# Wider up products, a fused clamp, an earlier first norm and a new fillers' table in a one-core mLSTM, gMLP and channel-mix kernel

## The chip, the cores and the metric

The kernel runs on one core of a Trainium2 chip. The metric is device time in microseconds (us); lower is better. The kernel before has a median of 297.68 us over three runs (297.44 to 298.55).

## The reference, cut to what matters

Three layers follow one another. B = 2 batches, S = 768 tokens, H = 8 heads of D = 40, so 320 features.

```python
# 1: mLSTM recurrence, per batch and head
m_new = max(f_gate + m, i_gate)
C = exp(f_gate + m - m_new) * C + exp(i_gate - m_new) * v k^T
n = exp(f_gate + m - m_new) * n + exp(i_gate - m_new) * k
y_t = sigmoid(o_gate) * (C q) / max(|n.q|, 1.0)
# 2: gated MLP over x = y laid out (B, S, 320)
h = relu(x @ w_in)                      # 320 x 1024
u, v = h[..., :512], h[..., 512:]
v_n = (v - mean(v)) / sqrt(var(v) + 1e-6)
x = (u * (w_spatial @ v_n + b_spatial)) @ w_out
# 3: channel mix
k = relu(mix_k(x) @ w_k)                # 320 x 1024
out = sigmoid(mix_r(x) @ w_r) * ((k * k) @ w_v)
```

## The kernel before, in words

The recurrence is computed in chunks of 128 tokens. There are 12 chunks (6 for each batch), taken in the order of `SEQ` = 0, 6, 1, 7, 2, 8, 3, 9, 4, 10, 5, 11: the two batches alternate, and two neighbours of `SEQ` are a **pair** (pair 1 is chunks 0 and 6, pair 6 is 5 and 11). The code counts pairs from g = 0. Names carry the chunk: `x11` is the x of chunk 11.

For one chunk the steps are: `scores` (k times q, tile `sc`), `logd` (the decay exponents, tile `ld`, whose Exp ScalarE takes into `dt`, which VectorE multiplies by `sc`), `inter` (q times the carried state, `ip`), `state` (the state's update, `sp` into `cn`), `intra` (`dt` times v, tile `av`; it ends in two halves, tasks N0 and N1), and `normalise`. That last one is a chain: `nn` plus `av` (line 626, VectorE; line 627, ScalarE, for each batch's first chunk), the output gate `og` times `nn` on GpSimd (line 622), the denominator `dn` on VectorE (lines 621, 629, 631), `x` = `og` times `dn` (line 632) and a copy of 64 columns on GpSimd (line 635). `turn` then transposes `x` on TensorE (tile `tp`, line 653), and ScalarE and VectorE split the result into a high and a low part in `xg`, one slot of three for each pair.

Products of layers 2 and 3 run in split precision: high times high, high times low and low times high, eight or so matmuls into one accumulator (line 678, function `mm3`). `upart(g)` makes the u half of pair g: four feature blocks of eight matmuls with 256 tokens moving; ScalarE applies the relu twice (once for each batch, line 771). `vpart(i)` makes the v half of one chunk with its normalisation: relu into `vr` (line 747; two buffers), statistics (735, 738), the 1e-6 (line 739, VectorE), the power -0.5 (line 744, GpSimd), for the first five chunks a bias (line 751, VectorE), scale, cast, and the low part on GpSimd into `vn`. Two PSUM banks (tag `mm`) hold these products and six (tag `at`) all else.

The order of work is laid down when the program is built. A planner with a clock of its own holds a list of tasks for each position p (slots S0, I, T, N0, X, S1, N1), takes the first of the next four whose inputs it believes ready, and after each task of slot s issues `FILL[p][s]` matmuls out of the **fillers** (`upart` and `vpart`). Where it sees a gap and has no filler it issues junk matmuls (`heat`, tile `wp`, line 378). `LATE`, `load`'s rates and the numbers in the chains are its estimates. Every engine then runs its list strictly in order, and TensorE's is fixed. What is left of the fillers after the last task is issued in one stretch, and then `spatial` (tile `spp`) starts, whose first call needs all six `vn` of batch 0 and whose weight halves come from GpSimd (`wsp`).

At the start, all loads go through SyncE's queue, whose order is spelt in two strings: `f i d q b o0 o1` (f and i gates, the identity, q and k of chunk 0, a mask, the output gates of chunks 0, 6, 1 and 7) and then `q6 k0 k6 v0 v1 v2 n` (q and k of chunk 6, k, v and q of chunks 0 and 6, w_u in three parts, q and k of chunk 1). `open_gate` takes the sigmoid of the output gates on ScalarE (line 370); the next Exp there needs a new table (ACT_TABLE_LOAD).

## Time and profile before

| | |
|---|---|
| median of three runs | 297.68 us (297.44 to 298.55) |
| the profiled execution, its own time | 296.37 us |
| its span, first to last instruction | 294.6 us |
| outside the span in that execution | 1.77 us |
| busy share of the span: TensorE, VectorE, ScalarE, GpSimd | 98%, 75%, 60%, 46% |
| recurrence and fillers, to the first spatial product | 0 to 119.1 us |
| the rest, layers 2 and 3 | 119.1 to 294.6 us |

Times inside a profile are counted from the span's first instruction. PE is TensorE's matmuls, PEld its weight loads, DVE is VectorE, ACT ScalarE, POOL GpSimd, SP SyncE. A matmul's own duration overlaps that of its neighbours, because they are pipelined; the time from the start of one to the start of the next is what a place in the list costs.

### The profile page before, as it was taken

The numbers are of one execution on the slowest core, as the hardware profiler recorded it, in microseconds if no ns is written. First come the engines' busy times: TensorE is split into PE (matmuls) and PEld (weight loads), VectorE is DVE, ScalarE is ACT, GpSimd is POOL, SyncE is SP. The second block draws the span as 40 slices with busy tenths as digits, with TensorE's granted clock in tenths as the row PEclk, the third lists the DMA queues.
The fourth block names the chain that finished last, engine by engine and source line by source line (L and its number), as shares of the span: only waits on it lengthen the run. The fifth ranks groups of instructions, "written<-read, shape, count | busy, mean of one in ns | idle before, by whom it ended". The sixth has DMA issues, their size and how long they took to land.

```text
span 294.6 us, 5892 instructions
## 1 busy us (share of the span) xinstructions
PE 288.9 (98%) x2167; PEld 265.2 (90%) x2167; DVE 221.3 (75%) x451; ACT 176.2 (60%) x385; POOL 134.5 (46%) x153
## 2 busy tenths in 40 slices
PE   8999999999999999999999999999999999999995
PEld 6777999888887889999999999898999899988994
DVE  6688898887778767366989989977986896556211
ACT  7676698947766456534454754694793788146400
POOL 5235426255776757424736526283812580045100
PEclk9999999999999999999999999999999999999999
DMA  6999697482412132462314302311102000100011
GB/s 153 312 233 299 179 296 211 108 234 77 128 49 74 53 92 62 162 191 103 89 47 148 112 6 83 93 43 44 49 0 87 4 0 22 47 22 1 2 45 46
DMA packets 14374, 29.53 MB, mean 100 GB/s; under 512 B 2641, under 2 KB 8017, under 8 KB 14345
## 3 DMA queue, kind: packets, MB, share of 16 engines
q1 hardware_dynamic: 14217, 29.09, 33.3%
q8 instruction: 17, 0.28, 0.4%
q0 software_dynamic: 128, 0.07, 0.2%
q14 instruction: 12, 0.10, 0.1%
HBM read 26.95 MB, written 1.97 MB: 98 GB/s over the span
## 4 chain that ended last, share of the span: by engine, by line
PE 82%; DVE 6%; ACT 5%; POOL 3%; DMA 2%; SPq 1%; issue 1%; DVEq 0%; POOLq 0%; ACTq 0%
PE spp L678 17%; PE kp L678 15%; PE vv L678 14%; PE up L678 8%; PE wop L678 8%; PE rp L678 5%; PE av L607 3%; PE vp L678 3%; PE sc L476 2%; PE ip L578 2%; DMA og<-in_o_tok_dram 2%; PE sp L541 1%; POOL vn L238 1%; DVE sb L735 1%; PE tp L653 1%
## 5 line engine op out<-in xcount | busy, mean ns | idle before, releaser
L678 PE MATMUL spp<-wsp,vn 128*128 128x384 f32 x288 | 50.4, 334 | 0.0
L678 PEld LDWEIGHTS spp<-wsp,vn 128*128 128x128 f32 x288 | 49.9, 188 | 0.0
L1238 POOL TENSOR_TENSOR sq<-sq 128x512 f32<-128x512 f32 x24 | 28.7, 1204 | 37.0 <-ACT sq L1237 37.0
L678 PE MATMUL kp<-xk,wk 128*128 128x512 f32 x192 | 44.3, 390 | 0.0
L678 PE MATMUL vv<-wv,k 128*128 128x320 f32 x288 | 42.7, 309 | 0.0
L678 PEld LDWEIGHTS kp<-xk,wk 128*128 128x128 f32 x192 | 35.9, 188 | 7.3
L678 PEld LDWEIGHTS vv<-wv,k 128*128 128x128 f32 x288 | 42.4, 188 | 0.0
L238 DVE TENSOR_TENSOR k<-sq,k 128x512 fp32r<-128x512 f32 x24 | 23.8, 993 | 9.6 <-ACT k L1239 8.6
L678 PE MATMUL up<-xg,w_u 128*128 128x256 f32 x192 | 29.3, 292 | 0.4 <-ACT u L771 0.4
L1122 POOL TENSOR_TENSOR vs<-vs,u 128x384 f32<-128x384 f32 x16 | 19.3, 1215 | 20.4 <-DVE vs L1121 20.4
L678 PE MATMUL vp<-w_v,xg 128*128 128x512 f32 x96 | 26.5, 407 | 0.0
L678 PEld LDWEIGHTS up<-xg,w_u 128*128 128x128 f32 x192 | 24.8, 190 | 1.7 <-ACT u L771 0.9
L678 PE MATMUL wop<-gt,wo 128*128 128x384 f32 x128 | 22.9, 334 | 0.0
L287 DVE SCALAR_TENSOR_TENSOR wbits<-wsq,wbits 128x320 int32<-128x320 int32 (+1 forms) x27 | 20.3, 753 | 3.0 <-ACT wsq L277 2.5
L1277 DVE TENSOR_TENSOR ob<-rs,vv 128x320 f32<-128x320 f32 x12 | 5.8, 488 | 22.3 <-PE vv L678 20.7
L678 PEld LDWEIGHTS wop<-gt,wo 128*128 128x128 f32 x128 | 22.3, 188 | 0.1
L1237 ACT ACTIVATE sq<-kp 128x512 f32<-128x512 f32 x24 | 14.2, 595 | 10.0 <-PE kp L678 10.0
L238 POOL TENSOR_TENSOR vn<-vr,vn 128x512 fp32r<-128x512 f32 x12 | 15.6, 1302 | 8.7 <-ACT vn L757 8.6
L678 PEld LDWEIGHTS vp<-w_v,xg 128*128 128x128 f32 x96 | 16.8, 189 | 2.9
L1175 DVE SCALAR_TENSOR_TENSOR tm<-x,mu_sb,tm 128x384 f32<-128x384 f32 (+2 forms) x36 | 18.2, 561 | 0.1
L1123 ACT CAST gt<-vs 128x384 fp32r<-128x384 f32 x16 | 8.2, 513 | 16.4 <-POOL vs L1122 15.4
L291 DVE SCALAR_TENSOR_TENSOR wsq<-wraw,wbits 128x320 int32<-128x320 int32 (+1 forms) x21 | 17.2, 823 | 0.4
(185 smaller groups left out, 573.1 us busy)
## 6 DMA issues: line engine op xcount, KB each, us to landing
kvq<-in_kvq_dram SPq DMA_DIRECT2D x10, 516.0 KB
qk<-in_qk_dram SPq DMA_DIRECT2D x23, 192.0 KB
wraw<-in_w_k_dram SPq DMA_DIRECT2D x6, 512.0 KB
wraw<-in_w_v_dram SPq DMA_DIRECT2D x8, 320.0 KB
wraw<-in_w_sp_dram SPq DMA_DIRECT2D x12, 192.0 KB
og<-in_o_tok_dram SPq DMA_DIRECT2D x12, 160.0 KB
out_dram<-ob SPq DMA_DIRECT2D x12, 160.0 KB
w_inu<-in_w_in_dram SPq DMA_DIRECT2D x3, 512.0 KB
```

Of the source, the lines that this page charges most:

```text
L238: eng.tensor_tensor(out=out, in0=a, in1=b.bitcast(F32), op=ALU.subtract)
L287: vec.scalar_tensor_tensor(out=t["bits"], in0=t["sq"].bitcast(I32), scalar=3, in1=t["bits"], op0=ALU.logical_shift_left, op1=ALU.bitwise_or)
L291: vec.scalar_tensor_tensor(out=t["sq"].bitcast(I32), in0=t["high"], scalar=SIGN, in1=t["bits"], op0=ALU.bitwise_and, op1=ALU.bitwise_or)
L476: pe.matmul(st["sc", i, x][:, h * P:(h + 1) * P], k_[64 * x:64 * x + D, h, :], q_[64 * x:64 * x + D, h, :], start=True, stop=True)
L578: pe.matmul(ip[:, h0 * DA:(h0 + n) * DA], qt[:n * D, g, :], cs[:n * D, h0 * DA:(h0 + n) * DA], start=True, stop=True)
L607: pe.matmul(av[r:r + 64, own_], A[:, h % 4, r:r + 64], vt[:, own_], start=True, stop=True)
L678: pe.matmul(out[0], l, x, start=j == 0, stop=j == len(prs) - 1)
L1122: ("P", 1.29, lambda: pool.tensor_tensor(out=vs, in0=vs, in1=ut[b][:, d, sl], op=ALU.mult)),
L1123: ("A", 0.51, lambda: act.copy(gt[:, 0], vs)), ("V", 0.7, lambda: sub(vec, gt[:, 1], vs, gt[:, 0])))
L1175: return lambda: vec.scalar_tensor_tensor(out=t[:, c], in0=x[:, c, lo + 1:hi + 1], scalar=mu_sb[:, w, c:c + 1], in1=t[:, c], op0=ALU.mult, ...
L1237: chain(("k2", g, f), ("A", 0.6, lambda: act.activation(out=sq, in_=ps, func=AF.Relu), ("kp", g, f)), ("P", 1.25, lambda: pool.tensor_tens ...
L1238: ("P", 1.25, lambda: pool.tensor_tensor(out=sq, in0=sq, in1=sq, op=ALU.mult)),
```

## The change

Five things change. (1) Pairs 3 and 4, and 5 and 6, are taken together by `upart(g, 2)`: 512 tokens move past one weight load instead of 256. For this all three slots lie in one tile `xall`, with neighbouring places for the pairs that go together; the products are issued at p = 8 and p = 12 instead of 6, 8, 10 and 12. The relu then covers 256 tokens of each batch. (2) The denominator is `|nn|` first, then its reciprocal, and the clamp to at most 1 is part of the multiplication into `x`: one VectorE instruction less for each chunk. The copy of `nn` for a first chunk goes from ScalarE to VectorE. (3) The addition of 1e-6 and the bias of the first five chunks go from VectorE to GpSimd. (4) At position 0 the second half of chunk 0 and its norm (N1) stand ahead of the second chunk's scores, and the loads are in another order. (5) The planner's estimates, `FILL` and `HOT` change.

```diff
-    LATE = dict(w_u0=0.5, w_u1=0.5, w_u2=0.5, w_v0=0.6, w_v1=0.6, w_v2=0.6)
+    LATE = dict(w_u0=0.7, w_u1=0.7, w_u2=0.7, w_v0=0.6, w_v1=0.6, w_v2=0.6)
...
-    for a in 'f i d q b o0 o1'.split():
+    for a in 'f i d o0 o1 q b'.split():
...
-            vec.tensor_scalar(out=spare, in0=nn[:, :, D], scalar1=1.0, scalar2=None, op0=ALU.max)
+            vec.scalar_tensor_tensor(out=spare, in0=nn[:, :, D], scalar=-1.0, in1=nn[:, :, D], op0=ALU.mult, op1=ALU.max)
...
-              ("A", 0.4, lambda: act.copy(nn, av)),
+              ("V", 0.4, lambda: vec.tensor_copy(nn, av)),
               ("V", 0.08, clip),
-              ("V", 0.15, lambda: vec.scalar_tensor_tensor(out=dn, in0=nn[:, :, D], in1=spare,
-                                                           scalar=-1.0, op0=ALU.mult, op1=ALU.max), ("av", i)),
-              ("V", 0.18, lambda: vec.reciprocal(out=dn, in_=dn)),
-              ("V", 0.4, lambda: vec.tensor_tensor(out=x[:, :DM].rearrange("p (h d) -> p h d", h=H), in0=osl,
-                                                   op=ALU.mult,
-                                                   in1=dn.unsqueeze(2).to_broadcast([P, H, D]))),
+              ("V", 0.18, lambda: vec.reciprocal(out=dn, in_=spare), ("av", i)),
+
+              ("V", 0.4, lambda: vec.scalar_tensor_tensor(out=x[:, :DM].rearrange("p (h d) -> p h d", h=H),
+                                                          in0=dn.unsqueeze(2).to_broadcast([P, H, D]), scalar=1.0, in1=osl,
+                                                          op0=ALU.min, op1=ALU.mult)),
...
+    xg, xall, XS = {}, [], (2, 0, 1)
...
+            xg[g] = xall[0][:, XS[g % 3]]
...
-                vec.tensor_scalar(out=sb[:, 8:9], in0=sb[:, 7:8], scalar1=1e-6, scalar2=None, op0=ALU.add)
...
+                pool.tensor_scalar(out=sb[:, 8:9], in0=sb[:, 7:8], scalar1=1e-6, scalar2=None, op0=ALU.add)
...
-                  *[("V", 0.1, lambda: vec.scalar_tensor_tensor(out=sb[:, 9:10], in0=sb[:, 6:7], scalar=-1.0, in1=sb[:, 8:9],
-                                                                op0=ALU.mult, op1=ALU.mult))] * early,
+                  *[("P", 0.2, lambda: pool.tensor_scalar(out=sb[:, 9:10], in0=sb[:, 6:7], scalar1=-1.0, scalar2=sb[:, 8:9],
+                                                          op0=ALU.mult, op1=ALU.mult))] * early,
...
+        x = xparts(xg[g], slice(0, 256)) if m == 1 else tuple(
+            [xall[0][:, XS[g % 3]:XS[g % 3] + 2, f] for f in fs] for fs in (range(3), range(3, 5)))
...
-    for a in 'q6 k0 k6 v0 v1 v2 n'.split():
+    for a in 'q6 k0 k6 v0 n v1 v2'.split():
...
-            (6, 2, 3, 8, 0, 4, 5, 10),
-            (7, 7, 1, 2, 2, 0, 0, 5),
+            (8, 0, 3, 9, 0, 2, 5, 11),
+            (9, 9, 1, 2, 2, 3, 0, 6),
...
-            if p % 2 == 0:
+            if p in (2, 4):
                 fillers.extend(upart(p // 2 - 1))
+            elif p in (8, 12):
+                fillers.extend(upart(p // 2 - 2, 2))
...
-            task(("S0", n), s0, after=[("N1", prev), ("S1", i)], arrive=n, slot=0, p=p)
+            task(("S0", n), s0, after=[("N1", prev), ("S1", i)] + [("N1", i)] * (p == 0), arrive=n, slot=0, p=p)
```

What the change does to the order is shown at three places.

SyncE's queue at the start, before and then changed: q and k of chunk 0 (`qk0`) and the four output gates.

```order
L388 DMA id_sb_80<-in_ident_dram 128x128
L219 DMA qk0_109<-in_qk_dram 48x1024 x2
L219 DMA bm_raw_105<-in_blockmask_dram 120x3x1
L219 DMA og0_0_113<-in_o_tok_dram 128x320
...
L219 DMA og1_1_119<-in_o_tok_dram 128x320
L219 DMA qk6_164<-in_qk_dram 48x1024 x2
```

```order
L388 DMA id_sb_80<-in_ident_dram 128x128
L219 DMA og0_0_109<-in_o_tok_dram 128x320
...
L219 DMA og1_1_115<-in_o_tok_dram 128x320
L219 DMA qk0_117<-in_qk_dram 48x1024 x2
L219 DMA bm_raw_105<-in_blockmask_dram 120x3x1
L219 DMA qk6_164<-in_qk_dram 48x1024 x2
```

The gates' four loads now stand ahead of q and the mask; from `qk6` on the order is as it was, up to w_u.

TensorE's list at the end of the recurrence, before and then changed, from the last `av` (chunk 11) to the transposes of chunks 5 and 11 and what follows them.

```order
L607 MATMUL av11_1657<-kvq11_1511,dt11_1_1608 64x41 x2
L678 MATMUL vp10_1652<-w_v0_670,xg4_1473 128x512 x2
L678 MATMUL vp10_1652<-w_v1_671,xg4_1473 128x512
L678 MATMUL up3_0_1693<-xg3_1175,w_u0_160 128x256
L678 MATMUL up3_0_1693<-xg3_1175,w_u1_161 128x256
L678 MATMUL up3_0_1693<-xg3_1175,w_u0_160 128x256 x2
L653 MATMUL tp5_1701<-id_sb_80,x5_1632 128x128 x3
...
L678 MATMUL up3_2_1729<-xg3_1175,w_u1_161 128x256
L678 MATMUL vp5_1743<-w_v0_670,xg5_1700 128x512
L653 MATMUL tp11_1746<-id_sb_80,x11_1684 128x128 x3
```

```order
L607 MATMUL av11_1632<-kvq11_1501,dt11_1_1594 64x41 x2
L680 MATMUL vp10_1638<-w_v0_659,xall_447 128x512 x2
L680 MATMUL vp10_1638<-w_v1_660,xall_447 128x512
L680 MATMUL vp10_1638<-w_v0_659,xall_447 128x512
L655 MATMUL tp5_1670<-id_sb_80,x5_1617 128x128 x3
L680 MATMUL vp10_1638<-w_v0_659,xall_447 128x512
L680 MATMUL vp10_1638<-w_v1_660,xall_447 128x512
L655 MATMUL tp11_1685<-id_sb_80,x11_1662 128x128 x3
L680 MATMUL vp5_1690<-w_v0_659,xall_447 128x512
```

Before, 20 up matmuls and one vp stand between the two transposes (the "..." leaves out 19 of the ups); now there are two vp matmuls. After `tp11` the list before holds 15 vp and 72 up matmuls of 256 tokens, the changed one 16 vp and 32 up matmuls of 512, and then `spp`.

VectorE's list at the same place, before and then changed (`nn11` plus `av11` to `x11`; `xg5` or `xall` from `tp5` is the low part of chunk 5's x).

```order
L626 TENSOR_TENSOR nn11_1645<-nn11_1645,av11_1657 128x328
L621 TENSOR_SCALAR av11_1657<-nn11_1645 128x8
L735 BN_STATS sb10_1691<-vr10_1690 128x6
...
L631 RECIPROCAL dn11_1683<-dn11_1683 128x8
L238 TENSOR_TENSOR xg5_1700<-tp5_1701,xg5_1700 128x2x128
L238 TENSOR_TENSOR xg5_1700<-tp5_1701,xg5_1700 64x128
L632 TENSOR_TENSOR x11_1684<-og5_1_766,dn11_1683 128x320
```

```order
L626 TENSOR_TENSOR nn11_1631<-nn11_1631,av11_1632 128x328
L621 SCALAR_TENSOR_TENSOR av11_1632<-nn11_1631 128x8
L629 RECIPROCAL dn11_1661<-av11_1632 128x8
L631 SCALAR_TENSOR_TENSOR x11_1662<-dn11_1661,og5_1_748 128x320
L238 TENSOR_TENSOR xall_447<-tp5_1670,xall_447 128x2x128
```

`x11` now stands ahead of the low part of chunk 5 and of chunk 10's statistics.

Over the whole list up to the first `spp`, TensorE changes from one kind of work to another 142 times before and 138 times now, and of the junk matmuls on `id_sb` 25 are left of 27.

## Rows read from the trace of the kernel before

**Rows 1.** The page, part 1: busy time of TensorE and its instructions.

```profile
PE 288.9 (98%) x2167; PEld 265.2 (90%) x2167; DVE 221.3 (75%) x451; ACT 176.2 (60%) x385; POOL 134.5 (46%) x153
```

**Rows 2.** Busy time by stage: stage and length, each engine's busy us, clock, DMA.

```profile
31.00:59.00 28.00, 28.00 (x350) 25.65 (x350) 25.30 (x63) 23.82 (x60) 10.97 (x15) 1.00 0.66 188
59.00:96.00 37.00, 36.56 (x331) 30.61 (x328) 29.91 (x85) 24.12 (x52) 24.33 (x31) 1.00 0.40 112
...
119.00:291.50 172.50, 172.17 (x993) 164.30 (x991) 125.79 (x197) 93.95 (x193) 70.74 (x62) 1.00 0.18 58
```

**Rows 3.** The chain that ended last: start us, us, what; fillers' rest and a 512-token product.

```profile
110.44 8.63 PE up L678 x72
...
224.57 14.53 PE kp L678 x64
```

**Rows 4.** Busy time by stage of the junk matmuls alone (tile wp).

```profile
12.00:31.00 19.00, 5.20 (x27) 1.00 0.99 295
```

**Rows 5.** The chain that ended last, 5 to 12 us.

```profile
5.04 4.48 DMA og<-in_o_tok_dram
...
9.54 0.47 ACT og L370
...
10.03 1.28 ACT L492
...
11.33 0.61 ACT dt L492
```

**Rows 6.** Timeline of TensorE, 8 to 12 us: start us, us, instruction, idle before and releaser.

```profile
8.97 1.16 PE L476 MATMUL sc<-qk 40*128 40x128 f32 x16
...
11.98 0.48 PE L484 MATMUL ld<-unit,Axa 128*128 128x512 f32 x1 [0.54 <-ACT dt L492]
```

**Rows 7.** Timeline of SyncE: issues of the first loads.

```profile
2.19 0.90 SPq L219 DMA_DIRECT2D qk<-in_qk_dram  x2
3.13 0.48 SPq L219 DMA_DIRECT2D bm_raw<-in_blockmask_dram  x1
3.66 1.81 SPq L219 DMA_DIRECT2D og<-in_o_tok_dram  x4
```

**Rows 8.** Timeline of GpSimd: the first use of a kvq load.

```profile
12.59 0.72 POOL L527 TENSOR_TENSOR kw<-kvq,ega 128x320 f32<-128x320 f32 x1 [5.74 <-ACT ega L440]
```

**Rows 9.** Timeline of TensorE at 95 us.

```profile
95.22 1.33 PE L678 MATMUL up<-xg,w_u 128*128 128x256 f32 x9 [0.44 <-ACT u L771]
```

**Rows 10.** Timeline of ScalarE ahead of that.

```profile
93.71 0.62 ACT L757 CAST vn<-vr 128x512 fp32r<-128x512 f32 x1 [1.90 <-DVE vr L755]
```

**Rows 11.** The chain that ended last: single stretches of TensorE.

```profile
37.40 0.52 PE up L678 x4
...
39.57 0.67 PE up L678 x4
...
102.12 0.91 PE vp L678 x3
...
106.46 0.22 PE tp L653 x2
```

**Rows 12.** Timeline of VectorE, 102 to 106 us.

```profile
102.95 0.48 DVE L626 TENSOR_TENSOR nn<-nn,av 128x328 f32<-128x328 f32 x1
...
104.89 0.68 DVE L238 TENSOR_TENSOR xg<-tp,xg 128x256 fp32r<-128x256 f32 x2
105.60 0.49 DVE L632 TENSOR_TENSOR x<-og,dn 128x320 f32<-128x320 f32 x1
```

**Rows 13.** Timeline of GpSimd, 103 to 107 us.

```profile
103.52 0.82 POOL L622 TENSOR_TENSOR og<-og,nn 128x320 f32<-128x320 f32 x1
...
106.22 0.42 POOL L635 COPY x<-x 128x64 f32<-128x64 f32 x1 [0.67 <-PE up L678]
```

**Rows 14.** Groups of instructions: count, busy us, mean ns, idle before: the small operations.

```profile
L739 DVE TENSOR_SCALAR sb<-sb 128x1 f32<-128x1 f32 x12 | 1.8, 154 | 0.4
...
L744 POOL TENSOR_TENSOR sb<-sb,eps 128x1 f32<-128x1 f32 x12 | 7.3, 611 | 8.0 <-DVE sb L739 7.4 <-DVE dn L631 0.7
```

More of the change, by code (lines that the diff above doesn't have):

```diff
@@ L227, in xslot @@
     def xslot(name, n):
-        return base.tile([P, 5 * 256], F32R, tag="xt", name=name, bufs=3)[:, :n]
+        return late_pool[0].tile([P, 5 * 256], F32R, tag="xt", name=name, bufs=3)[:, :n]
     def uslot(name, dt):
@@ L648, in turn @@
                 fill(1)
-            xg[g] = xslot(f"xg{g}", 5 * 256).rearrange("p (c t) -> p c t", c=5)
+            if not xall:
+                xall.append(at.tile([P, 3, 5, 256], F32R, name="xall"))
+            xg[g] = xall[0][:, XS[g % 3]]
         xt, ts = xg[g], slice(j * P, (j + 1) * P)
@@ L770, in relu @@
                         ut[b] = uslot(f"u{b}", F32).rearrange("p (d t) -> p d t", d=4)
+                    if m == 2:
+                        return lambda: act.activation(out=ut[b][:, d, c * P:(c + 2) * P].rearrange("p (m t) -> p m t", m=2),
+                                                      in_=ps.rearrange("p (m b t) -> p m b t", m=2, b=2)[:, :, b], func=AF.Relu)
                     return lambda: act.activation(out=ut[b][:, d, c * P:(c + 1) * P], in_=ps[:, b * P:(b + 1) * P], func=AF.Relu)
-                chain(("ut", c, d), ("A", 0.2, relu(0)), ("A", 0.2, relu(1)))
+                chain(("ut", c, d), ("A", 0.1 + 0.1 * m, relu(0)), ("A", 0.1 + 0.1 * m, relu(1)))
             w = wparts(W["u"], slice(d * P, (d + 1) * P))
-            r += mm3(lazy(lambda d=d: mm_bank(f"up{g}_{d}", ("ut", c, d))[:, :256]), pairs320(x, w, swap=True), after,
-                     ["w_u0", ("xt", c), ("xt", c + NCH)], 0.117, g, {3: ["w_u1"], 6: ["w_u2"]} if d == 0 else {})
+            r += mm3(lazy(lambda d=d: mm_bank(f"up{g}_{d}", ("ut", c, d))[:, :256 * m]), pairs320(x, w, swap=True), after,
+                     ["w_u0", *[("xt", c + o + n) for o in range(m) for n in (0, NCH)]], 0.117 if m == 1 else 0.226, g,
+                     {3: ["w_u1"], 6: ["w_u2"]} if d == 0 else {})
         return r
@@ L951, in s0 @@
             if p == 0:
-                heat(2)
+                heat(4)
             scores(n, 0)
@@ L981, in s1 @@
                 load_qk(SEQ[p + 3])
+            if p == 0:
+                w_in_load("v", 1, 0)
+                sync.dma_start(out=mu_sb, in_=mu)
             if p in (3, 5):
@@ L992, in n1 @@
                 load_kv(nn)
-            if p == 0:
-                w_in_load("v", 1, 0)
-                sync.dma_start(out=mu_sb, in_=mu)
             if p == 1:
@@ L1020, in position @@
             task(("N0", i), lambda: intra(i, 0), [("A", i, 0)], [("S0", i), ("N1", prev)], slot=3, p=p)
+            if p == 0:
+                task(("N1", i), n1, [("A", i, 0), ("A", i, 1)], [("N0", i), ("T", i)], slot=6, p=p)
         if prev is not None:
@@ L1024, in position @@
             task(("S1", n), s1, after=[("S0", n)], slot=5, p=p)
-        if i is not None:
+        if i is not None and p > 0:
             task(("N1", i), n1, [("A", i, 0), ("A", i, 1)], [("N0", i), ("I", i), ("T", i), ("S1", n), ("X", SEQ[p - 2] if p > 1 else None)], slot=6, p=p)
```

10 lines of the change are left out of this document (4 added, 6 removed), and 16 rows, old and new, of the table FILL.

## The prediction

> **What bounds the kernel now.** I read the busy shares first: TensorE is busy 288.9 of 294.6 us [rows 1], so the question is not which engine is the bound, but which of TensorE's time is work. The table by stage comes next [rows 2]: from 31 to 59 us TensorE has no idle time, from 59 to 96 us it has 0.44 us, and from 119 to 291.5 us next to none. Layers 2 and 3 are thus a fixed tail of some 175 us whose list does not change; whatever the change is worth must move the first spatial product, now at 119.07 us, where the fillers' rest of 8.63 us that starts at 110.44 ends [rows 3]. Then I looked for what is not useful work ahead of that point. There are 27 junk matmuls, 5.20 us busy [rows 4]. There are two waits: at 11.98 us TensorE has stood 0.54 us for an Exp [rows 6], and at 95.22 us 0.44 us for the relu of an up product [rows 9]. The reader is to see that a list this full has little to give back: about a microsecond of waits, and the work that the change itself takes off the list.
>
> **Wider up products.** Of the 192 up matmuls (6 pairs, 4 blocks, 8 each) the 64 of two pairs keep 256 tokens; the other 128 become 64 with 512. Where they run back to back, 72 of the old ones take 8.63 us, 0.120 each, and 64 matmuls of layer 3 with 512 tokens moving past the same kind of weights take 14.53 us, 0.227 each [rows 3]. So 128 x 0.120 = 15.34 becomes 64 x 0.227 = 14.53: **-0.8 us**. The bounds are 0 (the new operand is read in two pieces, which no row here shows) and -0.8. All of it is on TensorE's path. The Trainium skill (TensorE: Matmul & The Clock Gate, section Back-to-back issue gap) gives the gap of a single warm matmul as N/2.4 + 2.5 ns, 109 ns for 256 and 216 for 512; both lie under the rows, and by it this term would be -0.2 us, an estimate.
>
> **Junk.** Two fewer at 5.20/27 = 0.19 each [rows 4]: **-0.4 us**, if nothing waits in their place.
>
> **Changes of work.** TensorE's list changes from one kind to another 138 times instead of 142. What a change costs is seen in four up matmuls, 0.67 us straight behind `av` and 0.52 behind other work [rows 11], so 0.15 each: **-0.6 us**, with 0 as the other bound.
>
> **The start.** The 0.54 us wait goes back to a load: SyncE issues the gates' four loads from 3.66 to 5.47 [rows 7], the last lands at 9.54, its sigmoid takes 0.47, the table for Exp 1.28, and the Exp ends at 11.94; only then is a bank free for the second chunk's `ld` [rows 5, 6]. In the new order these loads are issued from 2.19, 1.47 us earlier, ahead of q's. That alone ends the first Exp at about 10.5, before TensorE asks for the bank (at 11.98 - 0.54 = 11.44): **-0.54 us**. What is late next: q of chunk 0 is now issued behind the gates. The same loads lie ahead of it as lay ahead of the last gate before, without the mask's, whose issue took 0.48 [rows 7], so it lands by about 9.54 - 0.48 = 9.06, where `scores` starts at 8.97 [rows 5, 6]; I take 0.0, and 0.57 as the other end, with the landing as it was. The norm of chunk 0 ahead of the second scores needs `kvq` of chunk 0, which had landed by 12.59, since what waited there was the Exp of the gates [rows 8]; TensorE comes to that `av` at about 12.5. If q is the later one, `scores` pays for it, but the Exp's wait stays away all the same. The instructions that move with it (the load of w_v's first part and of mu) are issued behind q and k of the next chunk, in a stretch in which no TensorE wait named a load; moving them is free while that holds, and costs their 1.5 us or so of transfer at the second pair if it does not.
>
> **The wait at 95 us.** It ended with an up product's relu, and ScalarE issued that behind a cast that had itself stood 1.90 us for VectorE in the chain of a chunk's v norm [rows 9, 10]. In the new order the relu of the first wide up block stands ahead of that cast, and a block lasts twice as long, so the bank has more time: **-0.44 us**, bounds -0.44 and 0.
>
> **VectorE and GpSimd.** One small VectorE instruction less for each norm and one for each v norm at 154 ns [rows 14], 24 in all, and five biases; two copies of 328 columns more, near the 0.48 us of the addition of that shape [rows 12]. About 3 us of VectorE go, none on the path while TensorE has no wait for it. GpSimd gets 12 additions and five biases of one column. Its nearest row is the power of the same size, 611 ns [rows 14]; the least is the 154 ns that VectorE takes. In the stage from 59 to 96 us, with some 15 of the 17, that is 2.3 to 9.2 us on top of 24.33 of 37 [rows 2]. I take 0 for the end: it fits in either way, and one change of engine (VectorE to GpSimd) falls out of every v norm.
>
> **The new end.** This is the term that speaks against the change. From the last `av`, which ends at 102.12, to the transpose of chunk 11 at 106.46, TensorE had 4.34 us of other work [rows 11]. Now it has four vp matmuls (0.91), a transpose (three matmuls, 0.11 each [rows 11], 0.33) and two vp (0.45): 1.7 us, so it arrives at 103.8. The wide products of pairs 5 and 6 can't fill in, since they need that very transpose. The chain of x for chunk 11 took: addition 102.95 to 103.43, gate on GpSimd 103.52 to 104.34, then VectorE was held by chunk 5's low part from 104.89, x 105.60 to 106.09, copy to 106.64 [rows 12, 13]. With the new order on VectorE x follows the gate directly: 104.4 to 104.9, copy to about 105.3. The first two transposes then wait 1.1 us and the third a little more, less the 0.2 from 106.46 to 106.64 that it waits now: **+1.0 us**. Bounds: +0.4, if the addition starts right behind `av`, and 106.46 - 103.8 = +2.6, if the chain is as late as it was. Behind it 32 x 0.227 = 7.3 us of up work still cover the v norm of chunk 5, which the first spatial product needs.
>
> **The sum.** -0.8 - 0.4 - 0.6 - 0.54 - 0.44 + 1.0 = -1.8 us. The profiled execution took 296.37 us (294.6 of span and 1.77 around it) and would take 294.6; the median of the runs is 297.68, 1.3 above that execution, and from it the change gives **295.9 us**, -0.6%.
>
> **Rivals.** (a) *The stall at the end is short* and the lead of the first stage is kept: the new wait at its bound of +0.4 and a little less stalling between, -2.4 to -3.3 us, 295.3 to 294.4. For it: most of VectorE's delays in the last chain are queueing, and its queue is shorter. Against: GpSimd's additions have to be made by someone. (b) *VectorE gives the lead back*: in the stage from 31 to 59 us it is busy 25.30 of 28.00 us [rows 2], and if TensorE arrives some 1.5 us early it may wait for `dt` and `xall` there until it is back where it was. Then only the last stage's -0.8 and the waits remain, with the new +1.0: -0.3 us, 297.4. Against it: the change takes work from VectorE. q landing late, -1.2 us, 296.5, falls in between. (c) *Slower*: GpSimd becomes the bound of the v norms. Two `vr` buffers let two norms be under way; the low part on GpSimd frees one. At 0.8 us for each small operation 15 of them take 12 us and GpSimd is busy 36.3 of 37; this decides from about 0.7 us each on. Each norm then comes about 1 us later, two under way, nine in the stage: +4.5 us, less what was won, +2.7, 300.4. The 611 ns say that it is near, and that the power is a costlier function than an addition says that it is not reached. (d) *A 512-token product costs no more than a 256-token one*: 64 x 0.120 would save 7.7 instead of 0.8, 289.0. The Trainium skill (same page and section) states about 131 ns for sustained 512-column products; the 64 at 0.227 [rows 3] say otherwise.
>
> **How the numbers follow.** The forecast (-1.0 to -2.3) has 0.50, (a) 0.20, (b) with late q 0.21, (c) 0.08, (d) 0.01. A median of this kernel tells about 0.5% (1.5 us) from no change. Faster by more takes (a), (d) and two thirds of the forecast: 0.54; slower takes (c) and a little of (b) where a load adds to it: 0.09; within, 0.37. The range leaves out the far end of (a), (c) and (d), and reaches to the no-change end of (b): 294.5 to 297.8 us.
>
> **What the profile will show.** Right: TensorE's group of 64 wide up matmuls starts one every 0.227 us; no idle time in front of `ld` at 11 to 12 us; first up product about 1 us earlier than 31.1; no wait for an up relu near 95 us; a wait of about 1 us in front of `tp` near the end, ended by x or its copy; first spatial product at about 117.3; the span from there on as before. Wrong: idle time of TensorE between 31 and 96 us, ended by VectorE or by ScalarE's `vr`; GpSimd's small operations at 0.7 us or more; `scores` later than 9.1; a stall of more than 2 us at the last transposes.

## The result, and the profile after

The changed kernel takes 301.19 us (median of six runs, 300.54 to 302.30) and the kernel before 297.56 us (296.92 to 298.55) on the same chip: a ratio of 1.0122, 95% interval 1.0097 to 1.0148. It is slower by 3.6 us where 1.8 us less were forecast. Medians in this document are over all runs of a kernel; the ratios and their intervals leave out its slow runs, those more than 1.5% above its fastest. The profiled execution spans 299.1 us, against 294.6 before. The first profile of the kernel before, with 296.37 us, lies 1.2 us under that median; a second one (b_again, below) spans 296.3 us. Both stand in this table, with the moments (us from the span's start) that the later argument uses.

| | before | before, second | after |
|---|---|---|---|
| first scores | 8.97 | 9.33 | 9.38 |
| first av | 14.62 | 14.79 | 13.28 |
| first up product | 31.09 | 31.26 | 31.15 |
| first v product | 59.26 | 60.50 | 60.99 |
| first spatial product | 118.92 | 120.18 | 122.30 |
| from first v to first spatial product | 59.7 | 59.7 | 61.3 |
| from first spatial product to the end | 175.7 | 176.1 | 176.8 |

The kernel before moves by itself: its two profiles differ by 1.2 us at the first v product. Against the second one, after loses 0.5 us up to the first v product, 1.6 us from there to the first spatial product and 0.7 us behind that, in what the prediction calls the tail; against the first one 1.7, 1.6 and 1.1 us.

The page of after, busy time of TensorE and the others, answers to [rows 1]; the table by stage to [rows 2]:

```profile
PE 289.7 (97%) x2101; PEld 261.6 (87%) x2101; DVE 223.6 (75%) x424; ACT 174.2 (58%) x367; POOL 140.4 (47%) x170
...
31.00:59.00 28.00, 27.24 (x319) 24.46 (x318) 25.75 (x59) 22.71 (x56) 13.20 (x16) 1.00 0.67 193
59.00:96.00 37.00, 35.26 (x327) 28.33 (x327) 26.15 (x63) 24.48 (x53) 26.20 (x41) 1.00 0.40 115
119.00:291.50 172.50, 171.56 (x980) 163.00 (x979) 130.80 (x201) 95.68 (x194) 75.41 (x67) 1.00 0.19 62
```

TensorE had no idle time from 31 to 59 us and 0.44 after it; now it has 0.76 and 1.74. The first of the two need not be the change's doing: the second profile of before has 1.03 us from 31 to 59 us. VectorE's busy time in the second stage fell from 29.91 to 26.15 us, but over the whole span it rose from 221.3 to 223.6; GpSimd's rose from 24.33 to 26.20 in that stage. TensorE's timeline shows the places:

```profile
9.38 1.54 PE L476 MATMUL sc<-qk 40*128 40x128 f32 x16
...
11.08 0.48 PE L484 MATMUL ld<-unit,Axa 128*128 128x512 f32 x1
...
20.57 0.27 PE L378 MATMUL wp<-id_sb 128*128 128x256 bf16 x1
21.63 0.68 PE L607 MATMUL av<-kvq,dt 128*64 128x60 f32 x16 [0.79 <-DVE dt L502]
...
87.30 1.18 PE L680 MATMUL vp<-w_v,xall 128*128 128x512 f32 x4
89.94 0.96 PE L680 MATMUL up<-xall,w_u 128*128 128x512 f32 x3 [1.47 <-ACT vr L749]
...
110.58 0.70 PE L655 MATMUL tp<-id_sb,x 128*128 128x128 f32 x3 [0.35 <-DVE x L631]
...
216.14 2.17 PE L680 MATMUL vv<-wv,k 128*128 128x320 f32 x13 [0.94 <-ACT sq L1248]
```

The wait for the Exp at 11 us is gone [rows 6], and so is that at 95 us [rows 9]. New are one for `dt` at 20.6 us, one of 1.47 us in front of the first wide product, 0.35 at the last transposes, and 0.94 us in layer 3. Here is what stands behind the wait at 88 us, on ScalarE, VectorE and GpSimd (three timelines of after):

```profile
80.58 0.60 ACT L749 ACTIVATE vr<-vp 128x512 f32<-128x512 f32 x1 [0.31 <-POOL vn L238]
83.08 0.60 ACT L749 ACTIVATE vr<-vp 128x512 f32<-128x512 f32 x1 [0.90 <-POOL vn L238]
85.41 0.82 ACT L755 ACTIVATE vr<-vr,sb 128x512 f32<-128x512 f32 x1 [1.33 <-POOL sb L753]
88.77 0.62 ACT L759 CAST vn<-vr 128x512 fp32r<-128x512 f32 x1 [1.40 <-DVE vr L757]
89.30 0.59 ACT L749 ACTIVATE vr<-vp 128x512 f32<-128x512 f32 x1
...
93.08 0.62 ACT L759 CAST vn<-vr 128x512 fp32r<-128x512 f32 x1 [1.47 <-DVE vr L757]
93.61 0.47 ACT L669 CAST xall<-tp 128x384 fp32r<-128x384 f32 x1
...
87.06 1.68 DVE L757 TENSOR_SCALAR vr<-vr,sb 128x512 f32<-128x512 f32 x1 [1.74 <-POOL sb L746]
...
81.77 1.28 POOL L238 TENSOR_TENSOR vn<-vr,vn 128x512 fp32r<-128x512 f32 x1 [1.22 <-ACT vn L759]
83.14 0.22 POOL L745 TENSOR_SCALAR sb<-sb 128x1 f32<-128x1 f32 x1
83.44 0.57 POOL L746 TENSOR_TENSOR sb<-sb,eps 128x1 f32<-128x1 f32 x1
83.97 0.82 POOL L622 TENSOR_TENSOR og<-og,nn 128x320 f32<-128x320 f32 x1
84.78 0.60 POOL L753 TENSOR_SCALAR sb<-sb 128x1 f32<-128x1 f32 x1
85.34 0.73 POOL L527 TENSOR_TENSOR kw<-kvq,egc 128x320 f32<-128x320 f32 x1
86.16 0.22 POOL L745 TENSOR_SCALAR sb<-sb 128x1 f32<-128x1 f32 x1
86.46 0.56 POOL L746 TENSOR_TENSOR sb<-sb,eps 128x1 f32<-128x1 f32 x1
86.98 0.23 POOL L634 COPY x<-x 128x64 f32<-128x64 f32 x1
87.17 1.29 POOL L238 TENSOR_TENSOR vn<-vr,vn 128x512 fp32r<-128x512 f32 x1
```

Read it backwards. The product needs the bank that the relu at 89.30 empties. That relu stands on ScalarE behind the cast of the norm before, the cast waits for VectorE's scale, and the scale, begun at 87.06, ends at 88.74, 0.28 us after GpSimd's subtraction for yet another norm. The same scale takes 0.53 us at 116.99 us, where it is not held up. Before it began, it had waited 1.74 us for GpSimd's power, and GpSimd had worked from 81.77 us on with no gap above 0.1 us. The reader is to see that three engines off TensorE's path, none busy for more than 71% of this stage, end TensorE's wait: a share over a stage hides the 6.7 us in which GpSimd is full.

### The profile page after: what moved, and what is told of

Read it like the earlier page. It is cut to its first block, busy times and chain, and to the rows that moved or that the text cites. A ratio compares the mean times of both kernels' runs of the same rounds, so it can differ in the third digit from the quotient of the medians.

```text
span 299.1 us, 5716 instructions
## 1 busy us (share of the span) xinstructions
PE 289.7 (97%) x2101; PEld 261.6 (87%) x2101; DVE 223.6 (75%) x424; ACT 174.2 (58%) x367; POOL 140.4 (47%) x170
## 4 chain that ended last, share of the span: by engine, by line
PE 61%; DVE 13%; POOL 7%; DMA 6%; ACT 6%; issue 5%; SPq 1%; DVEq 0%; ACTq 0%; POOLq 0%
PE spp L680 17%; PE vv L680 14%; PE kp L680 10%; PE wop L680 6%; PE up L680 4%; PE rp L680 3%; DMA w_inu<-in_w_in_dram 3%; PE vp L680 3%; DMA m<-mg 2%; POOL vn L238 1%; DVE k L238 1%; POOL sb L746 1%; DVE wsq L291 1%; DMA og<-in_o_tok_dram 1%; DVE tm L1186 1%
## 5 line engine op out<-in xcount | busy, mean ns | idle before, releaser
L238 DVE TENSOR_TENSOR k<-sq,k 128x512 fp32r<-128x512 f32 x24 | 26.1, 1091 | 7.9 <-ACT k L1250 6.9
L680 PE MATMUL up<-xall,w_u 128*128 128x256 f32 (+1 forms) x128 | 28.2, 353 | 1.6 <-ACT vr L749 1.5
L680 PE MATMUL vp<-w_v,xall 128*128 128x512 f32 x96 | 26.9, 411 | 0.1
L287 DVE SCALAR_TENSOR_TENSOR wbits<-wsq,wbits 128x320 int32<-128x320 int32 (+1 forms) x27 | 21.4, 794 | 6.8 <-ACT wsq L277 3.3
L680 PEld LDWEIGHTS up<-xall,w_u 128*128 128x128 f32 x128 | 20.2, 188 | 5.4 <-ACT vr L749 1.9
L1186 DVE SCALAR_TENSOR_TENSOR tm<-x,mu_sb,tm 128x384 f32<-128x384 f32 (+2 forms) x36 | 20.7, 619 | 0.1
L680 PEld LDWEIGHTS vp<-w_v,xall 128*128 128x128 f32 x96 | 16.8, 189 | 3.9 <-ACT xall L669 0.6
L238 POOL TENSOR_TENSOR vn<-vr,vn 128x512 fp32r<-128x512 f32 x12 | 15.4, 1287 | 7.1 <-ACT vn L759 7.1
L291 DVE SCALAR_TENSOR_TENSOR wsq<-wraw,wbits 128x320 int32<-128x320 int32 (+1 forms) x21 | 18.0, 859 | 0.3
```

Source lines behind the costliest of these rows:

```text
L238: eng.tensor_tensor(out=out, in0=a, in1=b.bitcast(F32), op=ALU.subtract)
L287: vec.scalar_tensor_tensor(out=t["bits"], in0=t["sq"].bitcast(I32), scalar=3, in1=t["bits"], op0=ALU.logical_shift_left, op1=ALU.bitwise_or)
L291: vec.scalar_tensor_tensor(out=t["sq"].bitcast(I32), in0=t["high"], scalar=SIGN, in1=t["bits"], op0=ALU.bitwise_and, op1=ALU.bitwise_or)
L680: pe.matmul(out[0], l, x, start=j == 0, stop=j == len(prs) - 1)
L1186: return lambda: vec.scalar_tensor_tensor(out=t[:, c], in0=x[:, c, lo + 1:hi + 1], scalar=mu_sb[:, w, c:c + 1], in1=t[:, c], op0=ALU.mult, ...
```

## The experiments

Two theories were set up first. **Order**: what TensorE is asked for, and when (the start, the table, the wide products), makes the waits. **GpSimd** (rival c in a small form): the small operations moved to GpSimd make the v norms late. All kernels of a group ran on one chip with the kernel before, whose medians there were 297.16 to 297.62 us. "after" and "before" name the kernel that is edited.

| run | median us | ratio to before, 95% interval |
|---|---|---|
| noD: after, small operations back on VectorE | 300.95 | 1.0066 to 1.0133 |
| noC: after, clamp and nn copy as before | 301.77 | 1.0093 to 1.0185 |
| noS: after, start and estimates as before | 319.11 | 1.0657 to 1.0763 |
| noB: after, narrow products | 301.62 | 1.0072 to 1.0177 |
| nlast: after, one load put back | 301.63 | 1.0079 to 1.0158 |
| noT: after, old table | 306.89 | 1.0220 to 1.0341 |
| b_wide: before, wide products alone | 300.73 | 1.0073 to 1.0135 |
| b_start: before, the start alone | 301.68 | 1.0095 to 1.0191 |
| b_clamp_ops: before, clamp and small operations alone | 305.38 | 1.0195 to 1.0295 |
| a_light, b_light: lighter loads of w_v, so other weights | 300.92, 296.89 | 1.0055 to 1.0156, 0.9945 to 1.0004 |
| b_again: before once more | 297.71 | 0.9965 to 1.0046 |
| a_bank: after, another bank at 88 us | 303.55 | 1.0110 to 1.0224 |
| a_nolow: after, GpSimd's part of the norm cut short, so left out of the result | 297.60 | 0.9979 to 1.0031 |
| a_wide34, b_wide34: pairs 5 and 6 narrow | 300.53, 298.54 | 1.0065 to 1.0145, 1.0002 to 1.0074 |
| a_lowV, b_lowV: that part on VectorE | 299.50, 299.05 | 1.0042 to 1.0109, 1.0024 to 1.0095 |

**One part undone: noD, noC, noS, noB, noT, nlast.** noD, noC and noB take the parts (3), (2) and (1) out of the changed kernel; noS takes (4) and the estimates out. In noD and noC TensorE's list is that of after, row for row.

> The changed kernel with the 1e-6 and the bias of the v norms back on VectorE; TensorE's list stays the same, row for row. Theory GpSimd (rival c of the prediction in a small form: each v norm passes GpSimd two more times, and VectorE's large operations run slower beside it): the wait of 1.63 us at 88 us and the longer VectorE operation of 1.68 us at 87.06 go, and the first spatial product comes about 1.6 us earlier, 299.5 us. Theory order (the waits follow from where TensorE's list and the start put things, not from who does the small operations): within 0.5 us of the changed kernel's 301.2.

> The changed kernel with the denominator as before (three VectorE instructions and a reciprocal ahead of x) and the copy of nn for the first two chunks on ScalarE; TensorE's list stays the same, row for row. Theory order: VectorE is late in the first 31 us since the norm of chunk 0 stands ahead of the mask product of chunk 6; the copy back on ScalarE takes 0.5 us off that, so the wait of 0.95 us at 20.6 falls by up to 0.5, and 12 small instructions of about 0.15 us come back on VectorE: 300.7 to 301.5. Theory GpSimd: no difference, 301.2.

> The changed kernel with the start as before: the loads in the old order, N1 of chunk 0 behind the second scores, w_v's first part behind N1, and the planner's old estimates. Theory order: the start gains 1.3 us and gives all of it back at 20.6, 28.1 and 32.5 us, and the waits at 37 to 38 and 59.6 us (about 1.2 us together) are its consequence too; without it the first up product stands near 31.1 as in both kernels and the first v product about 1.2 us earlier than 60.99: 300.0. The wait at 88 us stays. Theory GpSimd: nothing changes behind 31 us, 301.2 to 302.

> The changed kernel with pairs 3 to 6 as four narrow up products of 256 tokens, issued at positions 6, 8, 10 and 12 again; the table of fillers counts the same numbers, so that the order from 60 us on is another. Theory order in its form for the bank: the wait of 1.63 us at 88 us is that the first wide product finds no free bank because the v products were issued in one stretch ahead of it; with narrow products issued earlier it goes, and the wait of 0.5 us at the last transposes too, while 0.3 us of weight loads come back: 299.4. Theory GpSimd: the wait moves to another place of that stage and stays as large, 301.2 to 301.5.

```diff
-    for a in 'q6 k0 k6 v0 n v1 v2'.split():
+    for a in 'q6 k0 k6 v0 v1 v2 n'.split():
```

> The changed kernel with one entry of the second load string put back: q and k of chunk 1 behind w_u's three parts instead of between the first and the others. TensorE's list differs in one place of three matmuls. Theory load (that load waits for a q buffer until 10.95 us and holds SyncE's queue, so that w_u's parts 2 and 3 are issued at 11.79 instead of about 7.8; their splitting on VectorE, GpSimd and ScalarE is pushed from the idle time at 13 to 17 us into the stage from 20 to 36 us, where it makes x and dt late): the first matmul product behind 31 us stays, but the waits at 20.6, 37 and 38 us (about 1.9 us of excess together) go, first v product 1 us earlier than 60.99, 300.2 us. Theory table (the loss is what TensorE's list asks for and when): no change, 301.2.

> The changed kernel with the fillers' table and the hot places of before; wide products and the start stay as changed. Theory table: the changed table puts 13 v matmuls in one stretch at 71 us and 15 at 81 to 88 us with no up products between, so that the next product finds no bank; with the old table the wait of 1.63 us at 88 us goes and the stage from 59 us to the first spatial product is 1.5 us shorter: 299.7. Theory load: the waits of the start stay, the rest differs by chance only, 301.2 or more, since two junk matmuls come back.

None gives the loss back. noD, noC, noB and nlast stay within 0.7 us of after. In noC, noB and nlast the wait at 88 us is there again (1.34, 1.56 and 1.33 us, ended by `vr` on ScalarE); in noD it is split in two (timeline of TensorE):

```profile
83.41 0.72 PE L679 MATMUL vp<-w_v,xall 128*128 128x512 f32 x2 [0.88 <-ACT vr L748]
...
90.77 0.96 PE L679 MATMUL up<-xall,w_u 128*128 128x512 f32 x3 [0.47 <-ACT vr L748]
```

So neither the small operations nor the wide products alone are what makes it, and the theory GpSimd in this form falls. noC has one more thing to tell: the wait at 20.6 us is gone, and its first up product comes at 31.06 us all the same; at the last transposes it has 1.39 us of idle time instead of 0.35, since with the old denominator `x11` stands behind the low part of chunk 5 again (110.82 us instead of 110.02). noS and noT are worse by far than either theory had it: table and start belong together, so what either is worth alone these two can't say. noS also runs with a granted clock of 0.97 in the mean, with slices at 0.6 and 0.7.

**One part alone: b_wide, b_start, b_clamp_ops, b_again.**

> The kernel before with the wide up products alone (pairs 3 and 4, 5 and 6 together, issued at positions 8 and 12; start, clamp, small operations and table as before). TensorE's list is as before up to 88 us. Predicted from the trace of after: 64 wide products cost 15.84 us there and the 128 narrow ones 16.11 before, so -0.3; the last transposes wait as in the prediction, +0.5 to +1.0: 297.6 to 298.3 against 297.6. If the wide product were itself the cause (its bank is held twice as long), there is a wait of more than 1 us behind 88 us and 299 or more.

> The kernel before with the start alone (load order, N1 of chunk 0 ahead, w_v's first part moved, heat, estimates; products, clamp, small operations and table as before). Theory load: the loss of the first 60 us is all of the start's making, first v product at about 61 instead of 59.26 us, 299.3. Theory table: the start alone is neutral, 297.6, and what is lost behind it needs the new table.

> The kernel before with the fused clamp and the small operations on GpSimd alone; TensorE's list is the same but for two places of a few matmuls. Both theories: these two parts are not what makes the changed kernel slower, 297.3 within 0.8. If they were, 298.5 or more.

> The kernel before once more, for a second profile of it: the first stands 1.3 us below the median of the runs. If a span of about 295.6 shows its extra microsecond in TensorE's waits between 31 and 119 us, these waits come and go with small differences of the loads' landing in the kernel before too.

Each part alone costs more than the whole change does or nearly as much, and the forecasts missed it: b_wide stands 2.4 us above the range of its first one, and what its second one named, a wait for a bank, is not there; b_start stands 2.4 us above the higher of its two. In b_wide the list is the one of before up to 88 us; what is new stands at the last transposes (timeline of TensorE):

```profile
107.81 0.49 PE L655 MATMUL tp<-id_sb,x 128*128 128x128 f32 x3
111.08 0.88 PE L655 MATMUL tp<-id_sb,x 128*128 128x128 f32 x3 [2.78 <-DVE x L632]
```

In b_start TensorE stands 1.75 us at 58.2 us for a bank, for two junk matmuls that the planner put where it saw a gap, behind an up relu. b_clamp_ops missed its expectation by 7 us. Its stages show where most of that arises: in 27 to 31 us two waits on VectorE (1.07 us for `dt`, 1.17 us for `i`), and behind them a granted clock whose mean over 3 us lies between its two levels, 1.2 and 2.4 GHz (0.50 and 1.00):

```profile
24.00:27.00 3.00, 3.00 (x42) 2.40 (x41) 2.38 (x4) 1.59 (x4) 1.28 (x1) 1.00 1.07 330
27.00:30.00 3.00, 1.63 (x13) 1.07 (x9) 2.94 (x7) 1.09 (x3) 1.14 (x2) 1.00 0.93 315
30.00:33.00 3.00, 1.88 (x9) 1.72 (x10) 1.96 (x7) 1.00 (x2) 1.44 (x3) 0.77 0.73 253
33.00:36.00 3.00, 3.00 (x31) 2.39 (x30) 1.10 (x2) 0.85 (x4) 1.64 (x2) 0.66 0.48 119
36.00:39.00 3.00, 3.00 (x37) 2.82 (x37) 2.66 (x8) 1.67 (x7) 0.51 (x1) 1.00 0.11 26
```

Its first up product comes at 36.27 us, 5.0 us later than in the second profile of before. The v norms start only with the first v product (65.18 us in this run), so of its two parts it can only be the clamp with the copy of `nn` that makes these waits: ahead of the second one VectorE has the copy, 0.49 us, and `|nn|`, 0.81 us. That second profile of before has, as b_again was to show, a wait of its own at 48.49 us (1.03 us, for `lt`'s load), so a microsecond comes and goes in the kernel before too.

**Loads or engines: a_light, b_light.** The DMA engines are nearly full from 9 to 46 us, so a theory of loads was set against one of VectorE. The lines that repeat the 64 columns are left out here.

```diff
-            W[nm, "raw"].append((q, raw, load(raw, w_in[j, q], 512)))
+            W[nm, "raw"].append((q, raw, load(raw, w_in[j, q], 512) if nm == "u" else load(raw[:, :64], w_in[j, q, :, :64], 512)))
```

> The changed kernel with 64 of the 512 columns of each of w_v's three parts loaded (and repeated eight times for the splitting, so the v half is computed with other weights): 1.38 MB less to move between 21 and 41 us; the order of instructions on every engine is the same. Theory loads (the DMA engines are nearly fully busy from 9 to 46 us, eight loads of SyncE's queue are under way at most, and the recurrence waits there for kvq, rl and lt, so TensorE's lead at the start can't be kept and any change of order puts another load last): first v product at least 1.5 us earlier than 60.99 us, time 299.6 or less. Theory VectorE (VectorE, busy 25.75 of 28 us there and held up by GpSimd, sets the pace): the same as the changed kernel, 301.2.

> The kernel before with the same lighter loads of w_v. TensorE has 0.7 us of excess from 31 to 59 us there, so theory loads gives at most that and what of the start's 0.69 us at 11 us is a load's: 296.5 to 297.3. Theory VectorE: 297.3, no change.

The theory of loads falls as an account of the loss: a_light's first v product comes at 60.17 us, 0.8 earlier instead of 1.5 or more, the wait at 88 us stays (1.45 us), the stretch from there to the first spatial product is 61.3 us as in after, and the time is that of after within 0.3 us. b_light fits both theories.

**The wait at 88 us itself: a_bank, a_nolow, a_lowV, b_lowV.** The diffs, parts of lines, are the bank of one block (a_bank), and the last step of the norm in two ways (a_nolow, whose spatial products then read the high part twice, and the two lowV runs):

```diff
-mm_bank(f"up{g}_{d}", ("ut", c, d))
+(bank(psa, "at", f"up{g}_{d}", ("ut", c, d)) if (m, g, d) == (2, 2, 0) else mm_bank(f"up{g}_{d}", ("ut", c, d)))
...
-("P", 1.23, lambda: sub(pool, lo, vr, hi))
+("P", 1.23, lambda: sub(pool, lo[:, :8], vr[:, :8], hi[:, :8]))
...
-for t in vn[2 * b + s // 3])
+for t in [vn[2 * b + s // 3][0]] * 2)
...
-("P", 1.23, lambda: sub(pool, lo, vr, hi))
+("P", 1.23, lambda: sub(vec, lo, vr, hi))
```

> The changed kernel with one PSUM bank of the other six (tag at) for the first block of the first wide product, instead of one of the two of tag mm; the lists of all engines are the same, row for row. Theory bank (the wait of 1.6 us at 88 us, which stands at the same place in six profiles of kernels with the changed table, is TensorE waiting for the relu of a v product, which ScalarE has behind the cast of the norm before): the wait goes, and what it held up is 1.2 to 1.6 us earlier: 299.7 to 300.1. Theory pace (VectorE, GpSimd and ScalarE have no slack there, so a wait taken away at one place comes back at the next): the wait moves to behind 88 us, 300.9 to 301.3.

> The changed kernel with GpSimd's low part of each v norm cut to 8 of 512 columns, and the spatial products taking the high part in its place, so the output lacks the low part; the order on all engines is the same. GpSimd has some 1.2 us less to do for each of twelve norms and holds VectorE up less. Theory pace: the stage from 59 us to the first spatial product loses most of its waits, and layers 2 and 3 start with less behind: 299.0 or less. Theory bank alone: the wait at 88 us falls by the 1.15 us by which VectorE's scale was held up there, 300.1.

> The changed kernel with the low part of the twelve v norms on VectorE instead of GpSimd, issued at the same places; nothing left out. With the low part cut short the time was 297.6. Theory GpSimd in the norm (the subtraction of 1.28 us on GpSimd, behind which the small operations queue and which holds VectorE up, makes each norm too long for two buffers): the wait at 88 us and the one at 215 us go, VectorE takes 0.68 us more for each: 298.0 to 298.8. Theory pace of all engines (any work in the norm counts, wherever it is done): VectorE is later for x and dt in its place, 300 or more.

> The kernel before with the same move. Its norms just keep up: 0.6 us of excess at 94 us and 0.3 at 213 us in its second profile are what can be won. Theory GpSimd in the norm: 296.5 to 297.0. Theory pace of all engines: 297.3 to 299.

a_bank takes the wait away at 88.34 us, and a larger one comes at the next v product, in this execution with half the clock behind it (timeline, then stages):

```profile
88.34 0.86 PE L680 MATMUL up<-xall,w_u 128*128 128x512 f32 x3
...
94.17 1.83 PE L680 MATMUL vp<-w_v,xall 128*128 128x512 f32 x4 [1.71 <-ACT xall L669]
...
92.00:95.00 3.00, 1.29 (x5) 0.54 (x5) 2.97 (x7) 1.50 (x3) 1.99 (x2) 0.95 0.43 96
95.00:98.00 3.00, 3.00 (x19) 2.12 (x19) 2.79 (x8) 1.69 (x4) 2.36 (x5) 0.50 0.39 151
98.00:101.00 3.00, 3.00 (x10) 2.42 (x9) 1.88 (x2) 0.85 (x2) 2.52 (x4) 0.50 0.00 0
```

That v product starts at 94.17 us here and at 94.13 us in after: TensorE comes earlier and waits for `xall`, whose cast stands on ScalarE at 93.64 us (after: 93.61) behind the cast of the next norm, which waits for VectorE's scale in both. ScalarE, VectorE and GpSimd do the same from 85 to 94 us within 0.05 us. So the bank was where the wait showed, not its cause. Neither forecast holds (303.55 us, with an interval that overlaps that of after). a_nolow, with the order of every engine unchanged and about 1.1 us less for GpSimd in each norm (227 ns instead of 1287), brings the time back to that of before:

```profile
87.54 1.17 PE L680 MATMUL vp<-w_v,xall 128*128 128x512 f32 x4
88.55 0.86 PE L680 MATMUL up<-xall,w_u 128*128 128x512 f32 x3
...
59.00:96.00 37.00, 36.86 (x343) 30.53 (x342) 28.46 (x68) 26.30 (x55) 19.98 (x46) 1.00 0.40 118
119.00:216.00 97.00, 97.00 (x550) 94.20 (x549) 82.94 (x129) 54.35 (x113) 50.46 (x46) 1.00 0.29 90
```

TensorE's idle time in the stage from 59 us falls from 1.74 to 0.14 us, the first spatial product comes at 120.03 us, and the wait in layer 3 is gone. But it is not the same microseconds that come back. Its first v product is at 61.27 us, no earlier than in after, and from there to the first spatial product it takes 58.8 us, 0.9 less than the kernel before. The same cut in the kernel before was not run and might gain there too. So a_nolow shows that GpSimd's work in the norms holds after up, not that it is the difference between the two kernels. a_lowV, which leaves nothing out, lies between: it takes 60.7 us for that stretch and its first spatial product is at 122.11 us, nearly as late as after's, because the wait moved:

```profile
93.56 0.73 PE L680 MATMUL vp<-w_v,xall 128*128 128x512 f32 x2 [0.83 <-ACT xall L669]
94.83 0.74 PE L680 MATMUL vp<-w_v,xall 128*128 128x512 f32 x2 [0.54 <-DVE xall L238]
...
59.00:96.00 37.00, 35.55 (x329) 28.77 (x330) 29.92 (x71) 25.27 (x53) 17.48 (x35) 1.00 0.41 117
```

Its span is 1.3 us shorter than that of after, and 1.1 of it lies in the tail (no wait near 215 us); its median lies between the two forecasts. The same move makes the kernel before slower by 0.6%, which the theory GpSimd excluded: the wait that before has at 95 us (0.44 us, and 0.48 in its second profile) is 1.52 us there, and the stretch from the first v to the first spatial product takes 61.7 us instead of 59.7. So in the recurrence it is the pace of all engines, as the second theory had it: 0.7 us more for VectorE in each norm is not hidden in the kernel before either. What makes the wait in layer 3 is not shown: it is gone in a_nolow and a_lowV, where GpSimd has less to do, but also in noB, where it has not (175.7 us behind the first spatial product).

**The end: a_wide34, b_wide34.**

```diff
-            elif p in (8, 12):
-                fillers.extend(upart(p // 2 - 2, 2))
+            elif p == 8:
+                fillers.extend(upart(2, 2))
+            elif p in (10, 12):
+                fillers.extend(upart(p // 2 - 1))
```

> The changed kernel with pairs 5 and 6 as two narrow products again (issued at positions 10 and 12), pairs 3 and 4 wide. TensorE's list is the same up to the last transposes, between which 16 up matmuls of pair 5 now stand. Both theories: the wait at 88 us stays; the wait of 0.5 us ahead of the last transpose goes, 32 wide become 64 narrow for +0.1 to +0.4: 300.9 to 301.3.

> The kernel before with pairs 3 and 4 as one wide product at position 8, pairs 5 and 6 narrow. With all wide, the last transposes waited 3.2 us since nothing but those products was left to fill in. If that is what the wide products alone cost: 297.3 to 298.0, no wait at the last transposes. If the later issue of pair 3 costs it: 299 or more.

In both there is no wait at the last transposes. Both medians lie 0.4 to 0.5 us beside their forecasts. b_wide34 is 2.2 us faster than b_wide: most of what the wide products cost alone is that wait. a_wide34 gets 0.4 us to its first spatial product (121.88 us), and in its profiled execution layer 3 loses them again (span 299.1 us). b_wide34 takes 58.8 us from the first v to the first spatial product, 0.8 less than before, and loses it behind that, where TensorE stands 0.35 and 0.57 us at 135 us for a weight half of `spatial` (`wsp`). No version here is faster than the kernel before clear of noise.

## Why the prediction was wrong, by its steps

- **The step that failed** is the term "VectorE and GpSimd" at 0, with its reading that what is no wait of TensorE now is hidden: "none on the path while TensorE has no wait for it", and for the rest "Layers 2 and 3 are thus a fixed tail". A TensorE list without waits was taken for slack on the other engines. What the runs show in its place: from the first v to the first spatial product after loses 1.6 us, and its longest wait there, 1.47 us, goes back to the v norms (ScalarE, VectorE, GpSimd and back, two `vr` buffers). These have next to no slack in either kernel: 0.7 us more on VectorE in each norm costs the kernel before 0.6% (b_lowV), and 1.1 us less on GpSimd in each is worth 3.5 us to after (a_nolow, by the two ratios). The tail isn't fixed either: it is 1.1 us longer than in the first profile of before and 0.7 longer than in the second, with a wait of 0.94 us in layer 3.
- **The wait at 95 us, -0.44**: it went, and 1.47 us came at 88 us by the same mechanism, a relu behind a cast. The argument that "a block lasts twice as long, so the bank has more time" looked at the blocks behind the first; the first one takes its bank from a v product. noB, with narrow blocks, has the wait too (1.56 us).
- **The start, -0.54**: the Exp's wait went as described. The scores started 0.41 us later than in the first profile of before, but only 0.05 later than in the second, so that part is not the change's; they took 0.38 us longer than in both, which is what q cost, within the bound of 0.57. The first `av` came 1.34 us earlier, and all of it was given back by 31.15 us, as rival (b) has it; the first piece at 20.57 us, where `dt` stood on VectorE behind the norm of chunk 0. That piece alone decides nothing: noC has no wait there and is no earlier at 31 us.

```profile
19.43 1.55 DVE L631 SCALAR_TENSOR_TENSOR x<-dn,og 128x320 f32<-128x320 f32 x1 [0.46 <-POOL og L622]
20.90 1.27 DVE L502 TENSOR_TENSOR dt<-dt,sc 128x512 f32<-128x512 f32 x2
...
19.36 1.27 POOL L238 TENSOR_TENSOR w_u<-wsq,w_u 128x512 fp32r<-128x512 f32 x1
```

- **Wider products, -0.8**: from start to start the 64 take 15.84 us and the 128 took 16.11: -0.3. The last 32 back to back take 7.46 us in the chain, 0.233 each rather than 0.227, and the others stand between other work. So the term was mis-sized, inside its bounds. Rival (d) is out.
- **Junk, -0.4, and changes of work, -0.6**: 25 junk matmuls are left and are busy for 4.93 us instead of 5.20, so -0.3. No run prices the four changes of work. Together with the wide products these terms were to take 1.8 us of work off TensorE; its busy time is 289.7 us, against 288.9 before, so no such gain shows.
- **VectorE and GpSimd, the sizes**: taken out singly, parts (2) and (3) change nothing clear of noise in the changed kernel (noC, noD). But "about 3 us of VectorE go" is wrong: its busy time rose by 2.3 us. The groups of after:

```profile
L621 DVE SCALAR_TENSOR_TENSOR av<-nn 128x8 f32<-128x8 f32 x12 | 4.2, 348 | 0.3
...
L745 POOL TENSOR_SCALAR sb<-sb 128x1 f32<-128x1 f32 x12 | 3.0, 251 | 5.7 <-DVE sb L740 5.3
L753 POOL TENSOR_SCALAR sb<-sb 128x1 f32<-128x1 f32 x5 | 1.7, 335 | 0.3
L757 DVE TENSOR_SCALAR vr<-vr,sb 128x512 f32<-128x512 f32 x7 | 6.6, 939 | 5.2 <-POOL sb L746 5.2
```

  The moved operations take 251 and 335 ns, within the bounds and under rival (c)'s 0.7 us. The fused clamp saved VectorE no time: `|nn|` takes 348 ns in the mean (seven of the twelve about 182 ns, five 326 to 811) where the maximum with 1.0 took 172 and the removed instruction 156. The scale's mean rose from 614 to 939 ns, that of `x` from 662 to 802. What the clamp and the new order did gain is the shorter chain of `x11` at the end.
- **The new end, +1.0**: 0.35 us of idle time in after, close to the lower bound of +0.4 and on its condition: the addition starts 0.38 us after TensorE is through with the last `av` (108.24 to 108.62 us), where it took 0.83 before. With the old chain it is 1.39 (noC), and with the old table and chain 2.78 (b_wide), near the upper bound of 2.6.
- **The rivals**: the time is nearest to (c), 300.4, and the place is right, the v norms. Its cause is not: it blamed the length of the moved operations, and putting them back changes nothing (noD), so that its number is near is luck. (b) was right about the lead of the start.

What stays open: which part of the change uses up the margin that the norms have in the kernel before. The nearest suspect is the table. TensorE's idle time for `vr` or `u` between 62 and 98 us is 1.3 to 1.6 us in the profiles of after and of its variants with its table, its start and GpSimd's part of the norm whole (a_bank, which moves the wait, aside), with wide products and with narrow ones (noB); with the old table it is at most 0.8 us (before, b_start, b_wide, b_wide34, b_clamp_ops). But start and table could not be undone singly without larger losses, and the tables that would fit a single part were not searched for.

## What to carry to other kernels

A full list on the bounding engine, with no waits in it, says nothing of slack on the engines that feed it; before moving work, look for chains with few buffers that just keep up, and price the change there. A table of numbers fitted on the chip belongs to one exact program: each of the three parts tried alone cost 3 to 8 us under the old table, whatever it saved by itself. A wait that goes when its bank is changed may only move; take work out of the chain behind it before calling it the cause.

## What was not expected of the hardware

VectorE stands still beside GpSimd. The scale at 87.06 us took 1.68 us instead of 0.53, the x at 19.43 us 1.55 instead of 0.49, each until just after a GpSimd operation had ended (GpSimd was busy from 86.46 to 88.46 us without a break); of the twelve `|nn|`, which has two operands where the maximum had one, five were held up. The Trainium skill (SBUF — State Buffer, section Who interferes with whom) says that VectorE instructions with two SBUF inputs, and `tensor_scalar` in its fast mode, need ports shared with GpSimd, and that the engine that starts first has them for its whole instruction while the other is blocked. The traces agree in what is held up: the x and `|nn|` have two inputs, the scale is a `tensor_scalar`, and the maximum with one input stays at 171 ns in noC. They show one thing more: the scale began during a GpSimd copy of 0.23 us and stayed blocked through the next operation, of 1.29 us, as well. That the scale runs in the fast mode no run shows.

The granted clock fell to 0.50, the 1.2 GHz level, behind a wait of 1.71 us at 92.5 to 94.2 us (a_bank), and to means of 0.77 and 0.66 over 3 us each behind 1.07 and 1.17 us in close succession (b_clamp_ops). Behind the single 1.47 us of after it stayed at 1.00. A wait can thus cost more than its own length: of the 5.0 us by which the first up product of b_clamp_ops comes later, 2.5 us are idle time of TensorE from 27 to 33 us, and the lower clock of the slices from 30 to 36 us costs at most 1.7 us, an estimate (0.23 and 0.34 of 3 us).
